# A scheduler's prices and positions chosen anew in a one-core attention and feed-forward kernel

## The chip, the cores and the metric

The kernel runs on one core of a Trainium2 chip. The core has a matrix engine (TensorE, PE in the profile), a vector engine (VectorE, DVE), a scalar engine (ScalarE, ACT), a general engine (GpSimd, POOL) and a sync engine (SyncE, SP) that here issues nearly all DMA transfers. Each engine works through its own queue of instructions in a fixed order, and semaphores tie the queues together. The metric is device time in microseconds (us) of one execution; the less the better.

## The reference

Linear attention with a norm is followed by a feed-forward layer with softplus:

```python
# q, k, v: (8, 8, 576, 64) float32: batch, heads, positions, head width
kv = np.einsum('bhsd,bhse->bhde', k, v)
out = np.einsum('bhsd,bhde->bhse', q, kv)
rms = np.sqrt(np.mean(out * out, axis=-1, keepdims=True) + 1e-06)
attn = out / rms * g_norm
x = attn.transpose(0, 2, 1, 3).reshape(4608, 512)
h = x @ w_in                                  # w_in: (512, 2048), float64
g = np.maximum(h, 0.0) + np.log1p(np.exp(-np.abs(h)))
return g @ w_out                              # w_out: (2048, 512), float64
```

## The kernel before

Tokens are cut into 36 tiles of 128. For each of the 8 batches `kv_of` loads K and V in pieces and multiplies them (line 691), and for each tile `rows` transposes q (line 771 on PE for the first two batches, line 746 on DVE for the others), multiplies it with kv (line 715), squares on ACT, sums on DVE (719), takes the root on POOL (722, 723) and scales on DVE (727). The result is transposed back on PE (733) for the first 12 tiles and on DVE for the others, and stored to DRAM.

Matrix products of the feed-forward layer keep float32 precision by splitting each operand into three pieces of a shorter format, so that a product is three passes. x is split by `split` (ACT line 635, DVE 638 and 641). Weights come as float64, 512 KB a piece; DVE and ACT turn them into float32 (lines 429 to 459) and split them (496 to 524, where lines 520 and 521 are on PE for the first four chunks). The 2048 hidden columns are 16 chunks of 128.

The feed-forward work has two forms. The narrow form (`step`) takes blocks of three tiles (384 tokens): 12 blocks, four chunks each for the first four blocks and six for the rest, 64 steps. A step is one first product (line 858, 12 matmuls), softplus and split on ACT and DVE (880, 882, 869, 873), and three second products (line 865, 3 matmuls each). The wide form (`wide_step`) does the remaining chunks over 512 tokens at a time in 48 steps, by a scheme that needs seven products where eight would be needed (line 1060, 6 matmuls each), with ACT copies and one DVE addition (line 1109) between them and eight second products (line 1130, 3 matmuls each). Its inputs are prepared by `units_of` (loads at line 989, kept at 970), its weights by `both`.

None of this is issued in program order. Every operation is first a task: `add` names its engine, a price in ns, the tasks that it waits for, buffers taken and given back, a transfer size for DMAs and a position. `Plan.order` plays the tasks through a simple model of the engines and the DMA queue. At each turn an engine looks at the tasks that could start within SOON of its first and takes the one with the lowest position; the resulting starts give the order in which all instructions are issued. The prices and positions therefore make no work, but set the order in every queue. What else the model has:

- HANDOVER: what passes between the end of a task on an engine and the start of one that waits for it; SWITCH: what PE pays extra from one kind of visit (rows, kv, all the rest) to another.
- `behind`: a gate. A load waits until the first product at or before that position has been done. A negative gate is none.
- `spare`: while the seventh first product has not started, PE's gaps of 400 ns or more are filled with matmuls that compute nothing (line 1224).
- P0 to P7: the positions. FETCH and CONVERT are the first eight weights' loads and conversions, P4 the tiles, P5 the batches' kv and q, P1 and P2 the later weights, P3 the offsets inside a wide step, P6 the unit loads.

Four load buffers of 256 KB hold K and V (ring e); one buffer each holds a raw piece of w_in and of w_out; two PSUM banks (ring h) hold the narrow first products.

## Time and profile before

| | |
|---|---|
| Median of 3 runs (lowest to highest) | 869.35 us (868.46 to 869.48) |
| The profiled execution | 869.26 us, span 867.5 us |
| Instructions | 17041 |
| DMA | 167.07 MB, mean 193 GB/s over the span |
| Granted TensorE clock, mean | 1.000 |

The span runs from the first instruction to the last. "Busy" is the time in which an engine executes at least one instruction; matmuls overlap, so the mean duration of one is longer than the pitch at which they start. PEld is the weight load of PE, which overlaps the matmuls. Line numbers are those of the kernel before. An "idle before" names what ended the wait.

### The profile page before, as it was taken

Reading aid. Unit: us, or ns where it says so; the run is one execution under the profiler, and the core shown is the slowest. Engines: PE = TensorE matmul, PEld = TensorE weight load, DVE = VectorE, ACT = ScalarE, POOL = GpSimd, SP = SyncE. Lnnn points to the kernel's source line nnn. Section 1 sums busy time; section 2 is a strip of 40 time slices with the busy share of each in tenths; the row PEclk is TensorE's granted clock in tenths of the full one; section 3 lists DMA queues with packets and bytes.
Section 4 is the critical chain, followed back from the end, with each engine's and each line's share of the span. In section 5 each row is a group of like instructions: output and inputs, shape, how many; then the busy total and the mean of one; then the engine's idle time right before and its main releaser. Section 6 shows DMA issues by size and latency. Waiting matters only on the chain.

```text
span 867.5 us, 17041 instructions
## 1 busy us (share of the span) xinstructions
PE 853.9 (98%) x6464; PEld 760.3 (88%) x6464; DVE 704.4 (81%) x995; ACT 521.3 (60%) x980; POOL 76.6 (9%) x79
## 2 busy tenths in 40 slices
PE   7899999999999999999999999999999999999998
PEld 5678888898888999989999999998999899999996
DVE  7888898888788879798887798878788666788873
ACT  6866664445444467766667655654868555566654
POOL 0342223111113200000000000000000000000000
PEclk9999999999999999999999999999999999999999
DMA  9998998779773655436645546545364752777764
GB/s 278 285 242 230 244 262 255 172 224 234 211 188 114 180 175 166 145 108 209 210 156 164 168 151 205 188 144 170 122 201 140 230 165 91 241 236 241 242 190 126
DMA packets 239778, 167.07 MB, mean 193 GB/s; under 512 B 106320, under 2 KB 198736, under 8 KB 239696
## 3 DMA queue, kind: packets, MB, share of 16 engines
q1 hardware_dynamic: 239392, 165.86, 64.5%
q8 instruction: 50, 0.82, 0.4%
q14 instruction: 32, 0.26, 0.1%
q10 hardware_dynamic: 304, 0.13, 0.1%
HBM read 112.98 MB, written 52.95 MB: 191 GB/s over the span
## 4 chain that ended last, share of the span: by engine, by line
PE 94%; DVE 1%; ACT 1%; POOL 0%; issue 0%; ACTq 0%; DVEq 0%
PE banks L1130 31%; PE banks L1060 28%; PE banks L865 16%; PE banks L858 15%; PE banks L715 2%; PE banks L691 2%; PE banks L733 0%; DVE units L638 0%; DVE half L727 0%; PE banks L1224 0%; POOL roots L723 0%; DVE units L641 0%; DVE roots L719 0%; DVE m L459 0%; ACT units L635 0%
## 5 line engine op out<-in xcount | busy, mean ns | idle before, releaser
L1130 PE MATMUL banks<-pieces,gv 128*128 128x512 f32 x768 | 239.9, 394 | 0.0
L1130 PEld LDWEIGHTS banks<-pieces,gv 128*128 128x128 f32 x768 | 133.5, 189 | 18.4
L1130 PE MATMUL banks<-pieces,g_False 128*128 128x512 f32 x384 | 149.4, 389 | 0.0
L858 PE MATMUL banks<-units,pieces 128*128 128x384 f32 x768 | 145.4, 337 | 0.0
L865 PE MATMUL banks<-pieces,gv 128*128 128x512 f32 x576 | 144.9, 396 | 0.0
L858 PEld LDWEIGHTS banks<-units,pieces 128*128 128x128 f32 x768 | 135.5, 188 | 4.8
L865 PEld LDWEIGHTS banks<-pieces,gv 128*128 128x128 f32 x576 | 106.1, 188 | 20.3
L1060 PEld LDWEIGHTS banks<-units,pieces 128*128 128x128 f32 x840 | 112.8, 190 | 6.8 <-ACT banks L1105 0.4
L1060 PE MATMUL banks<-units,pieces 128*128 128x256 f32 x840 | 117.1, 282 | 0.0
L880 ACT ACTIVATE half<-banks 128x384 f32<-128x384 f32 x64 | 31.4, 491 | 98.2 <-PE banks L858 98.0
L1120 DVE TENSOR_TENSOR gv<-g_True,gv 128x1024 fp32r<-128x1024 f32 x47 | 57.5, 1223 | 37.8 <-ACT gv L1117 37.8
L1130 PEld LDWEIGHTS banks<-pieces,g_False 128*128 128x128 f32 x384 | 72.2, 188 | 15.9
L1060 PEld LDWEIGHTS banks<-units,w 128*128 128x128 f32 x504 | 67.8, 190 | 3.9 <-ACT banks L1105 0.2
L1060 PE MATMUL banks<-units,w 128*128 128x256 f32 x504 | 70.7, 282 | 0.0
L723 POOL TENSOR_TENSOR roots<-roots,half 128x8 f32<-128x8 f32 x36 | 62.3, 1731 | 3.0
L1123 DVE SCALAR_TENSOR_TENSOR g_False<-gv 128x1024 fp32r<-128x1024 f32 x47 | 57.6, 1225 | 1.5
L1109 DVE TENSOR_TENSOR g_True<-banks,g_True 128x512 f32<-128x512 f32 x48 | 33.1, 690 | 30.5 <-PE banks L1060 24.5
L1087 ACT ACTIVATE g_True<-banks 128x256 f32<-128x256 f32 x96 | 36.6, 382 | 32.8 <-PE banks L1060 32.2
L1023 DVE TENSOR_TENSOR units<-loads,units 128x1024 fp32r<-128x1024 f32 x42 | 51.2, 1219 | 6.3 <-ACT units L1020 6.3
L925 ACT ACTIVATE m<-banks 128x512 f32<-128x512 f32 x72 | 42.1, 595 | 19.8 <-PE banks L1130 13.8
L1026 DVE SCALAR_TENSOR_TENSOR units<-units 128x1024 fp32r<-128x1024 f32 x42 | 51.4, 1224 | 1.8
L869 DVE TENSOR_TENSOR gv<-half,gv 128x384 fp32r<-128x384 f32 x64 | 35.4, 553 | 20.6 <-ACT gv L882 19.9
(115 smaller groups left out, 1260.5 us busy)
## 6 DMA issues: line engine op xcount, KB each, us to landing
loads<-x SPq DMA_DIRECT2D x180, 128.0 KB, 2.6
part<-m SPq DMA_DIRECT2D x72, 256.0 KB, 2.9
m<-part SPq DMA_DIRECT2D x72, 256.0 KB, 3.2
loads<-form SPq DMA_DIRECT2D x45, 256.0 KB, 3.2
form<-loads SPq DMA_DIRECT2D x36, 256.0 KB, 3.0
raw<-in_moe_w_in_dram SPq DMA_DIRECT2D x16, 512.0 KB, 4.5
loads<-in_k_dram SPq DMA_DIRECT2D x32, 256.0 KB, 4.1
loads<-in_v_dram SPq DMA_DIRECT2D x32, 256.0 KB, 4.4
```

The costliest lines, as they stand in the source:

```text
L723: nc.gpsimd.tensor_tensor(out=r.tile, in0=r.tile, in1=half, op=ALU.pow)
L858: nc.tensor.matmul(hp, lhsT=w_in.tile[:, i, kd * P:(kd + 1) * P], rhs=xv.tile[:, i, kd], start=(m == 0), stop=(m == 3 * KD - 1))
L865: nc.tensor.matmul(mine[i].tile, lhsT=gv.tile[:, m, i * P:(i + 1) * P], rhs=w_out.tile[:, m], start=(c == cs[0] and m == 0), stop=(c == cs ...
L869: nc.vector.tensor_tensor(out=gv.tile[:, 1], in0=g.tile, in1=gv.tile.bitcast(F32)[:, 0], op=ALU.subtract)
L925: a = add("ACT", 690 if ph == LAST else 600, lambda: nc.scalar.activation(new(ot, [P, d_model]), bank.tile, func=AF.Copy, scale=scale if p ...
L1023: nc.vector.tensor_tensor(out=part_of(1, F32R), in0=xl.tile if m > 1 else xl.tile[:, 0], in1=part_of(0), op=ALU.subtract)
L1026: nc.vector.scalar_tensor_tensor(out=part_of(2, F32R), in0=part_of(1), scalar=-RADIX, in1=part_of(0), op0=ALU.mult, op1=ALU.add)
L1060: nc.tensor.matmul(place(q), lhsT=w[:, m, at:at + P], rhs=dst.tile[:, m, v, kd] if u < 6 else dst.tile[:, m, kd], start=(u == 0 and not m ...
L1087: nc.scalar.activation(dst, src, func=AF.Softplus, scale=1.0 + E)
L1120: nc.vector.tensor_tensor(out=gvt(1, F32R), in0=gt(), in1=gvt(0), op=ALU.subtract)
L1123: nc.vector.scalar_tensor_tensor(out=gt(F32R), in0=gvt(1), scalar=-RADIX, in1=gvt(0), op0=ALU.mult, op1=ALU.add)
L1130: nc.tensor.matmul(mine[i].tile, lhsT=(gvt(m, F32R) if m < 2 else gt(F32R))[:, c, i * P:(i + 1) * P], rhs=outs[c].tile[:, m], start=fresh ...
```

## The change

The planner's model of prices changes, and the positions are replaced. No task is added or taken away, apart from the number of fill matmuls that the planner chooses.

- HANDOVER gives way to two figures: a task occupies its engine for `busy`, which on ACT and DVE is less than its price, and is seen by others after `lag`; REACH is added on the side of the waiting engine.
- SWITCH knows four forms of dense visit (mm1, mm2, prod, all) and prices each change between them and rows or kv. PE prefers to stay in a form by 0.5 of a position.
- Prices of PE tasks, SP issues (460 ns for most) and transfer sizes are new, and SOON is 60 instead of 150, the fill 260 instead of 400.
- A new list P8 gives positions of their own to the split and the overflow sum of the first eight weights, the stores of the first 12 tiles and the second products of the first 16 narrow steps.

The diff, cut to its core (price changes of the same kind are left out; of the lists only P0, P3, P4, P5 and P6 are shown; P1, P2 and P7 are replaced in the same manner, and P8 has 44 entries):

```diff
-    HANDOVER = {"PE": 250, "ACT": 120, "DVE": 120, "POOL": 150, "SP": 0}
+    OVERLAP = {"ACT": (250, 60, 105), "DVE": (200, 40, 90)}
+    SEEN = {"PE": 0, "ACT": 33, "DVE": 33, "POOL": 34, "SP": 0}
+    REACH = {"PE": 190, "ACT": 0, "DVE": 0, "POOL": 55, "SP": 0}
     READY = {"PE": 2500, "ACT": 2500, "DVE": 4000, "POOL": 2500, "SP": 700}
-    SWITCH = {("all", "rows"): 90, ("all", "kv"): 90, ("rows", "all"): 250, ("kv", "all"): 250, ("rows", "kv"): 140, ("kv", "rows"): 140}
+    SWITCH = {("prod", "mm2"): 17, ("mm1", "mm2"): 30, ("mm2", "mm1"): 30, ("rows", "kv"): 60, ("kv", "rows"): 100}
+    for form in ("mm1", "mm2", "prod", "all"):
+        SWITCH.update({("rows", form): 260, ("kv", form): 290, (form, "rows"): 10, (form, "kv"): 10})
+    STAY = 0.5
-    LANDING, FILLED = 3500, 60000
+    LANDED, LANDING, FILLED = 1300, 3500, 60000
+    QUEUED = 3000
-    SOON = 150
+    SOON = 60
...
+        limit, short, long = self.OVERLAP.get(engine, (0, 0, 0))
+        t.busy = ns - (long if ns > limit else short)
+        t.lag = ns - t.busy + lag + self.SEEN[engine]
...
-                        at = max(at, dma_free - 2500)
+                        at = max(at, dma_free - self.QUEUED)
...
-                at, t = min(options, key=lambda o: (o[1].pos, o[0]))
+                at, t = min(options, key=lambda o: (o[1].pos - (self.STAY if engine == "PE" and o[1].kind == "all" and o[1].form == form else 0), o[0]))
...
-            engine_free[t.engine] = at + t.ns
-            t.end = at + t.ns + self.HANDOVER[t.engine]
+            engine_free[t.engine] = at + busy
+            t.end = at + busy + t.lag
...
-                t.end = dma_free + (self.LANDING if dma_free > self.FILLED else 2000)
+                t.end = dma_free + (self.LANDING if dma_free > self.FILLED else self.LANDED)
...
-                    u.ready = max([a.end for a in u.after] + ([u.follows.start] if u.follows else []), default=0)
+                    u.ready = max([a.end + self.REACH[u.engine] for a in u.after] + ([u.follows.start] if u.follows else []), default=0)
...
-    P0 = [-45.94, -26.77, -11.8, 0.28, -29.91, -5.64, -2.86, 3.84, -103.4, -98.98, -69.3, -76.66, -68.5, -24.67, -23.22, -34.97, 8.15, -43.02, 7.47, 9.69, 7.18, 18.16, -12.1, 4.75, 1.0, 106.19, 31.3, 6.28, 7.19, 5.22]
-    P4 = [-30.17, -6.08, 16.93, -33.9, -22.35, -28.91, -17.33, -7.12, -18.68, -2.69, 0.62, 2.73, -7.38, -1.86, 1.1, 1.72, 5.22, -13.65, 3.22, 0.88, 43.88, 43.95, -0.17, -0.32, 44.8, 40.82, -20.17, -6.56, 6.41, 10.03, -10.73, 0.23, 2.8, 0.42, -9.48, -5.03]
-    P5 = [1.24, -5.69, -2.28, -3.57, 1.72, 0.53, 6.68, -5.83, 3.01, -2.95, 3.35, 1.4, -6.96, 0.27, -5.34, -2.29]
+    P0 = [-68.7, -102.34, -44.82, -198.78, -249.41, -62.35, -115.05, 6.21, -525.68, -256.69, -299.97, -218.24, -570.6, -112.98, -68.54, -94.85, -20.21, -104.06, 52.6, 12.02, 30.74, 101.38, -89.91, 0.87, 2.46, 290.7, 63.96, 11.88, 7.87, 7.29]
+    P4 = [-106.62, -49.32, -12.94, -239.17, -63.65, -156.56, -38.04, -130.43, -253.55, -40.59, 8.15, -36.8, 140.03, -108.31, -11.51, 403.76, 8.82, -40.31, 56.72, -0.01, 294.4, 87.55, 118.45, -23.98, 191.1, 161.79, 101.83, -115.05, 18.29, -158.32, -176.64, 0.8, -4.24, -184.6, -64.73, 82.92]
+    P5 = [-65.91, -22.31, -22.19, 41.72, -93.2, -155.53, 98.26, 0.78, 50.55, -63.11, -38.66, 4.6, -5.42, 20.99, -30.64, -2.0]
-    P6 = [1.05, 6.24, 4.29, 4.08, -1.52, -2.85, 1.21, -0.34, 3.11, 3.1, -1.07, -0.73, -0.88, 9.99, 5.7, 5.69, 0.13, 0.46]
+    P6 = [18.97, 22.66, -6.96, -0.88, -33.45, -44.23, -110.04, 16.54, 29.17, -20.75, 14.92, -72.25, -181.54, 3.37, -1.25, -197.59, -239.43, -207.09]
...
-    P3 = [2.14, 2.48, 6.41, -16.53, 0.86, 2.79, 4.01, -16.44, 3.79, 3.96, 2.19, 1.79, 0.72, 1.35, 1.55, -1.03]
+    P3 = [7.03, 2.4, 10.2, -70.67, 2.74, -26.0, 4.18, -42.87, -107.53, 2.93, -129.46, 1.88, -15.26, -256.2, 14.29, 9.63]
...
-        f = add("SP", 450, fetch, (), fetch_pos, [raw], size=1800, behind=behind)
+        f = add("SP", 460, fetch, (), fetch_pos, [raw], size=2250 if of_out else 1750, behind=behind)
...
-            divide(j, w, ready, pos, c < 4)
+            divide(j, w, ready, pos + (P8[j] if c < 4 else 0), c < 4)
...
-            b2 = add("PE", 500, less_by_pe, [e], pos, [bank])
+            b2 = add("PE", 334, less_by_pe, [e], pos, [bank], lag=92)
...
-            lds = [add("SP", 500, lambda src=src, s=s, load=load: load(src, s), (), pos - EARLY[6] + 0.5 * p + (P7[2 * (5 * b + p) + of_v] if b < 2 else 0), [s], [],
-                       650 if tail else 850, behind=pos - 5.5) for of_v, (src, s) in enumerate(((k, ks), (v, vs)))]
+            lds = [add("SP", 460, lambda src=src, s=s, load=load: load(src, s), (), pos - EARLY[6] + 0.5 * p + (P7[2 * (5 * b + p) + of_v] if b < 2 else 0), [s], [],
+                       640 if tail else 930, behind=pos - 5.5) for of_v, (src, s) in enumerate(((k, ks), (v, vs)))]
...
-            last = add("PE", 470, run, lds + ([last] if b < 2 else []), pos + 0.5 * p, [bank] if p == 0 else [], [ks, vs], kind="kv",
+            last = add("PE", 467, run, lds + ([last] if b < 2 else []), pos + 0.5 * p, [bank] if p == 0 else [], [ks, vs], kind="kv", lag=209,
...
-        a = o_task = add("PE", 484, out_rows, turned + need, x_pos(t - second), [o], [qT], kind="rows", follows=rows_done.get(t - 1))
+        a = o_task = add("PE", 515, out_rows, turned + need, x_pos(t - second), [o], [qT], kind="rows", follows=rows_done.get(t - 1), lag=240)
...
-        a = add("PE", 2100, mm1, x_split[n] + factors_done[0, c] + [m for _, m in mm1s[-1:]] +
+        a = add("PE", 2092, mm1, x_split[n] + factors_done[0, c] + [m for _, m in mm1s[-1:]] +
                 (factors_done[1, ORDER[s - 2][1]] if s > 1 else []), s, [h],
-                ([xv] if c == cs[-1] else []) + ([w_in] if s == last_step[c] and c != 4 else []))
+                ([xv] if c == cs[-1] else []) + ([w_in] if s == last_step[c] and c != 4 else []), lag=41, form="mm1")
...
-            a2 = add("PE", 700, lambda i=i: mm2(i), [a] + factors_done[1, c] + [mm2s.get(i)], s + 1.5,
+            a2 = add("PE", 684, lambda i=i: mm2(i), [a] + factors_done[1, c] + [mm2s.get(i)], s + 1.5 + (P8[28 + s] if s < 16 else 0),
                      [mine[i]] if c == cs[0] else [],
-                     [gv] + ([w_out] if s == last_step[c] and not kept else []))
+                     [gv] + ([w_out] if s == last_step[c] and not kept else []), form="mm2")
...
-            return add("PE", 710, lambda: product(u, q), unit_done[ph, n, u] + forms_done[p][f] + list(after), pos, take, give,
-                       follows=follows)
+            return add("PE", 716, lambda: product(u, q), unit_done[ph, n, u] + forms_done[p][f] + list(after), pos, take, give,
+                       follows=follows, lag=83, form="prod")
...
-    plan.spare = ("h", warm, 400, mm1s[6][1])
+    plan.spare = ("h", warm, 260, mm1s[6][1])
```

## The prediction

> **What bounds the kernel now.** I read the page first: the engines' busy shares and the shares of the chain that ended last.
>
> ```profile
> span 867.5 us, 17041 instructions
> ...
> PE 853.9 (98%) x6464; PEld 760.3 (88%) x6464; DVE 704.4 (81%) x995; ACT 521.3 (60%) x980; POOL 76.6 (9%) x79
> ...
> PE 94%; DVE 1%; ACT 1%; POOL 0%; issue 0%; ACTq 0%; DVEq 0%
> ```
>
> TensorE (PE) is busy 98% of the span and is 94% of the chain. But busy says nothing of useful: next the busy times by stage (columns: window, length, PE, PEld, DVE, ACT, POOL busy with counts, granted clock, DMA share, GB/s), and behind them the first row again for line 1224 alone, the fill matmuls, which compute nothing.
>
> ```profile
> 0.00:80.00 80.00, 70.17 (x904) 54.20 (x905) 67.93 (x119) 54.51 (x106) 24.15 (x29) 1.00 0.96 256
> 80.00:300.00 220.00, 220.00 (x2104) 196.76 (x2103) 188.32 (x323) 111.99 (x223) 52.46 (x50) 1.00 0.78 212
> 300.00:850.00 550.00, 550.00 (x3390) 497.90 (x3389) 443.53 (x547) 348.91 (x643) 0.00 (x0) 1.00 0.56 178
> 850.00:867.50 17.50, 13.71 (x72) 11.41 (x70) 4.60 (x8) 5.92 (x11) 0.00 (x0) 1.00 0.40 124
> ```
> ```profile
> 0.00:80.00 80.00, 18.86 (x52) 10.77 (x52) 1.00 0.96 256
> ```
>
> From 80 to 850 us PE has no idle at all. In the first 80 us it is idle 80 - 70.17 = 9.8 us and fills for 18.86: 28.7 us without use. The last 3.8 us are the last copy and store.
>
> Is the packed part at its least? The chain gives the pitch of each kind of visit (start, us, what):
>
> ```profile
> 192.74 2.10 PE banks L858 x12
> 194.84 2.08 PE banks L865 x9
> ...
> 442.42 2.87 PE banks L1060 x24
> 445.30 2.75 PE banks L1130 x12
> ```
>
> So the narrow first product (768 matmuls) takes 64 x 2.10 = 134.4 us, the narrow second one (576) 64 x 2.08 = 133.1, the wide first one (2016) 84 x 2.87 = 241.1, the wide second one (1152) 96 x 2.75 = 264.0. PE's timeline gives the small visits, and what changing costs:
>
> ```profile
> 108.38 2.27 PE L858 MATMUL banks<-units,pieces 128*128 128x384 f32 x12
> 110.58 1.16 PE L715 MATMUL banks<-early,w 64*64 64x64 f32 x64
> 111.67 4.42 PE L865 MATMUL banks<-pieces,gv 128*128 128x512 f32 x18
> 115.93 2.27 PE L858 MATMUL banks<-units,pieces 128*128 128x384 f32 x12
> 118.13 1.15 PE L691 MATMUL banks<-loads 128*64 128x64 f32 x32
> 119.21 0.69 PE L715 MATMUL banks<-early,w 64*64 64x64 f32 x32
> 119.83 2.35 PE L858 MATMUL banks<-units,pieces 128*128 128x384 f32 x12
> ```
>
> Start to start, two tiles of rows (x64) take 1.09, two kv visits (x32) 1.08: 36 rows make 19.6, 40 kv visits 21.6; 22 transposes at some 0.38 and 8 pairs of lines 520 and 521 at some 0.55 (the same timeline, before 80 us) 12.8. The sum is 826.6. With 1.6 us before the first matmul and 3.8 behind the last it is 832.0 of 867.5. Of the 35.5 left, 27.1 are the start's (28.7 less that 1.6). The other 8.4 are changes of visit: the dense visits beside a small one take 0.10 too much on either side (108.38 to 110.58 is 2.20, not 2.10; 111.67 to 115.93 is 4.26, not 4.16), so 0.2 for each of some 43 stays of small work, 18 of them after 80 us.
>
> What holds the start? DVE works 67.93 of the first 80 us, and its own timeline shows it packed:
>
> ```profile
> 35.44 0.68 DVE L719 TENSOR_REDUCE roots<-half 128x8 f32<-128x512 f32 x1
> 36.03 0.68 DVE L442 SCALAR_TENSOR_TENSOR m<-sq,m 128x512 f32<-128x512 bf16 x1
> 36.63 0.68 DVE L727 TENSOR_TENSOR half<-banks,roots 128x512 f32<-128x512 f32 x1
> ```
>
> These start every 0.60, while the planner before charged 690 and a handover of 120. DVE's least before the last second product of the first block: 8 weights x (0.43+0.69+0.69+0.43+0.69+0.69+0.72) = 34.7, 3 tiles x 4 x 0.69 = 8.3, 4 steps x 1.1 = 4.4, after the first landing at 4.36: 51.8 us. That product ended near 79; the rest of DVE's time went to later tiles. Of its 12.1 us idle, 2.6 lie before that landing, 9.5 behind it, in pieces of 0.1 to 1.3 waiting for ACT, PE and POOL. The first dense visit shows how a fixed order loses time: its tile was split by 40.7, but PE takes two small visits and six fills, 42.96 to 44.44, first.
>
> **The change part by part.** No instruction is added or removed but fills; what changes is the order in each queue, computed from new prices and positions. Which order comes out can't be read from the diff, so each part is bounded.
>
> Prices of DVE and ACT: they are now occupied 40 to 105 ns less than an operation lasts. That is what the rows above show (0.60 for 0.68). Over the 119 DVE operations of the first 80 us the old plan charged some 0.09 too much each, 10.7 us, and so gave DVE's queue and PE's fills an order for a slower start. What a truer order can win by packing alone is DVE's 9.5 us of idle time; what it can lose is one weight's way, 5.8 us from issue to landing. I take a gain of 4.5, half of the idle time: no row says how many pieces had other ready work.
>
> Fills: 260 instead of 400 ns, so shorter gaps are filled and there will be more than 52 of them. A fill at pitch 0.23 delays what is ready behind it. Between the six before the first dense visit gone (-1.5) and a dozen more that come late (+2.8) I take 0; the cover is that DVE, not PE, is late there.
>
> Changes: to rows and back is charged 270 instead of 340, to kv and back 300. Four stays merged or split at 0.2 give -0.8 to +0.8; I take 0, since the price hardly moves.
>
> Gates and transfers: worked from the new positions, K/V loads of batches 4, 5 and 6 lose their gates (behind narrow steps 10, 13, 23 before, now none), and so do q of batch 3 and many loads of units. They can come into the start, past the weights on SP. Only four load buffers of 256 KB exist: 1.05 MB, 4.1 us at the 256 GB/s above, is the most. I take 0, as their positions (39, 46, 76) stand behind every weight fetch of the start (-68 at the latest); ends 0 and +4.1. SP issues as many DMAs as before, at some 0.46 each; the larger transfer prices move no data.
>
> Packed part, 80 to 850: 0. A gain is excluded beyond the changes; a loss is the second rival. Tail: 0.
>
> Sum: -4.5 against the profiled execution's 869.26 (span 867.5 and 1.8 around it; 0.09 below the median) gives 864.8, against the median 864.9. I say **865**, and 0.2% (1.7 us) is what a measurement can tell from no change.
>
> **The rivals.**
>
> *A load held on SP in the start (slower, chance 0.17).* SP issues in order. A load placed early whose buffer comes free late holds the weights and K/V behind it, then DVE, then PE. For it: the open gates, a landing now priced 1300 instead of 2000 before 60 us, the start's DMA share of 0.96. Against: SP's longest wait in the first 80 us is 2.9 us, and PE waits for K/V only 0.2 to 1.7 at a time. It decides once a weight is later than DVE's idle pieces hide, about 1 us. Price: a landing of 4.1 to 5.8 us less that, some 4: 873. [...]
>
> *The wide steps lose their cover (slower, 0.11).* Positions of the second products and of the product after DVE's addition move by up to 250 steps. That addition (0.69 us at line 1109, and ACT's copies at some 0.37) stands between two products, and second products of the step before hide it. If they are used up too soon, PE waits some 0.2 us in each of 48 steps: 9.6 us, 879. For it: 550 us rest on this order. Against: in each 10.5 us step 5.5 us of second products cover some 1.5 us. It decides below two of them between the last two products.
>
> *No change (0.10).* The start is held by transfers, at 0.96 of the DMA engines; another order moves the same bytes: 869. Against: DVE waits for a landing 1.8 us in all. [...]
>
> *More than packing (faster, 0.16).* DVE's work for later tiles is put off, toward its 51.8 us: as the start then gives up to twice the 4.5, some 859.
>
> **How the numbers follow.** My forecast has 0.46, with its own range 861 to 867.5. Faster: 0.46 + 0.16 = 0.62; same 0.10; slower 0.17 + 0.11 = 0.28. The range runs from 858, which leaves out half the bigger gains (0.08), to 876, which leaves out the wide-step case (0.11).
>
> **What would show it.** Right: the first dense visit before 44.4 us; fills and idle together under 25 us in the first 80; DVE over 70 us busy there; no idle PE from 80 to 850; some 18 stays after 80. Wrong: PE idle at K/V or weights in the start, or gaps at lines 1060 and 1130 in the wide steps.

## The result and the profile after

The changed kernel is slower: 875.35 us median of 6 runs (875.15 to 875.73) against 869.41 us for the kernel before (6 runs beside it, 868.46 to 870.48). The ratio is 1.0068, 95% interval 1.0055 to 1.0081. The forecast was 865.0, range 858 to 876: the time fell inside the range, but on the other side of no change.

Line numbers of the changed kernel are those of the kernel before plus 12 wherever this text needs them: 691 is 703 (kv), 715 is 727 (rows), 733 is 745 (turn of x), 858 is 870 (narrow first product), 1224 is 1236 (fill). The profiled execution took 875.72 us. From the page of the changed kernel, the span, the busy shares and the chain:

```profile
span 873.9 us, 17082 instructions
PE 861.9 (99%) x6501; PEld 764.2 (87%) x6501; DVE 688.8 (79%) x995; ACT 515.5 (59%) x980; POOL 80.8 (9%) x79
PE 92%; DVE 2%; ACT 2%; DMA 1%; POOL 1%; SPq 1%; issue 1%; DVEq 0%; ACTq 0%
```

PE is busy for 8.0 us more, DVE for 15.6 us less. There are 37 fills more (89 for 52), each a matmul and a weight load, and 33 semaphore instructions less, which makes the 41 instructions more. Busy times by stage (window, length, then PE, PEld, DVE, ACT, POOL busy with counts, granted clock, DMA share, GB/s), and the first window again for the fills alone (line 1236):

```profile
0.00:80.00 80.00, 73.92 (x809) 58.48 (x810) 62.83 (x114) 50.65 (x100) 20.78 (x25) 1.00 0.94 242
80.00:300.00 220.00, 217.94 (x2207) 193.93 (x2207) 180.21 (x316) 111.79 (x221) 60.00 (x54) 1.00 0.78 213
300.00:850.00 550.00, 550.00 (x3380) 494.89 (x3379) 437.02 (x555) 342.90 (x642) 0.00 (x0) 1.00 0.56 178
```
```profile
0.00:80.00 80.00, 27.14 (x89) 17.34 (x89) 1.00 0.94 242
```

In the first 80 us PE is idle for 6.08 us and fills for 27.14: 33.2 us without use, where it was 28.7. From 80 to 300 us another 2.06 us are idle, where there were none. Together that is 6.6 us, and the last product ends 6.4 us later than before (870.09 against 863.71). So nearly the whole loss is in the start and just behind it; the wide steps, from 300 to 850 us, have no idle time, as before.

What the start hangs on shows in PE's timeline (start, busy, line, operation, idle time before and its releaser): K/V visits of batch 0, the first rows, one K/V visit of batch 1, the first dense visit.

```profile
14.82 0.69 PE L703 MATMUL banks<-loads 128*64 128x64 f32 x16
20.03 0.69 PE L703 MATMUL banks<-loads 128*64 128x64 f32 x16
24.68 0.69 PE L703 MATMUL banks<-loads 128*64 128x64 f32 x16
28.01 1.16 PE L727 MATMUL banks<-early,w 64*64 64x64 f32 x64
45.45 0.69 PE L703 MATMUL banks<-loads 128*64 128x64 f32 x16 [0.66 <-DMA loads<-in_v_dram]
50.29 2.03 PE L870 MATMUL banks<-units,pieces 128*128 128x384 f32 x10
```

The first three lines are the second to fourth K/V visits of batch 0. The same visits, the first rows and the first dense visit in the kernel before:

```profile
9.57 0.69 PE L691 MATMUL banks<-loads 128*64 128x64 f32 x16
...
15.32 0.69 PE L691 MATMUL banks<-loads 128*64 128x64 f32 x16
...
19.30 0.69 PE L691 MATMUL banks<-loads 128*64 128x64 f32 x16 [1.69 <-DMA loads<-in_k_dram]
...
21.44 1.16 PE L715 MATMUL banks<-early,w 64*64 64x64 f32 x64
...
44.44 2.28 PE L858 MATMUL banks<-units,pieces 128*128 128x384 f32 x12
```

The K/V visits are 4.7 to 5.4 us later, the first rows 6.57, the first dense visit 5.85. The queue of SP shows the reasons (start, time the issues took, line, tile, count):

```profile
10.53 2.59 SPq L773 DMA_DIRECT2D w<-in_q_dram  x4
13.16 2.25 SPq L773 DMA_DIRECT2D early<-in_q_dram  x4
15.54 0.43 SPq L692 DMA_DIRECT2D loads<-in_k_dram  x1
...
17.72 0.50 SPq L692 DMA_DIRECT2D loads<-in_v_dram  x1
...
31.52 3.99 SPq L625 DMA_DIRECT2D early<-in_q_dram  x2
35.57 5.39 SPq L773 DMA_DIRECT2D w<-in_q_dram  x2
41.05 0.45 SPq L810 DMA_DIRECT2D x<-w  x1
41.62 0.99 SPq L692 DMA_DIRECT2D loads<-in_v_dram  x2
```

Four q loads (eight DMAs, for two half tiles and two whole ones) go ahead of the last K piece (15.54) and V piece (17.72) of batch 0. In the kernel before, all K/V pieces of that batch are issued by 12.21 us:

```profile
10.14 0.45 SPq L680 DMA_DIRECT2D loads<-in_k_dram  x1
10.65 0.98 SPq L680 DMA_DIRECT2D loads<-in_v_dram  x2
11.82 0.34 SPq L418 DMA_DIRECT2D g<-in_moe_w_out_dram  x1
12.21 0.42 SPq L680 DMA_DIRECT2D loads<-in_k_dram  x1
```

The eight issues take 4.84 us of SP's time. The K piece behind them then lands 3.23 us after its own issue, while the one issued at 12.21 in the kernel before took 6.96; so its place behind these issues made it late more than a full queue of transfers did. The second K/V visit is late for a reason of its own: its V piece is issued at 8.79 us (before at 4.30), behind two weight pieces (5.93 and 7.71). The V piece at 17.72, too, stands behind two of them (16.08 and 17.30).

Later, from 32 to 41 us, three issues take 3.45, 3.53 and 1.81 us; the median of the 810 issues on SP in this trace is 0.43. The V piece behind them is issued at 41.62 and lands at 45.41, where PE has been waiting for it.

Behind 80 us there is one new gap of more than 0.3 us: the turn of x at 89.55.

```profile
89.55 0.63 PE L745 MATMUL banks<-ident_r,half 128*128 128x128 f32 x4 [1.45 <-DVE half L739]
```

Two sums of the planner belong to this picture; they are plans, not measurements. The changed kernel's planner, with its new prices, ends the last product of its own order at 866.2 us. Given the order of the kernel before, the same prices end it at 871.7. So by its own prices the change gains 5.5 us. On the chip the old order ended at 863.7, 8.0 ahead of that plan, and the new one at 870.1, 3.9 behind it.

### The profile page after: what moved, and what is told of

It reads as the page before. It is cut to its first block, busy times and chain, and to the rows that moved or that the text cites. A ratio compares the mean times of both kernels' runs of the same rounds, so it can differ in the third digit from the quotient of the medians.

```text
span 873.9 us, 17082 instructions
## 1 busy us (share of the span) xinstructions
PE 861.9 (99%) x6501; PEld 764.2 (87%) x6501; DVE 688.8 (79%) x995; ACT 515.5 (59%) x980; POOL 80.8 (9%) x79
## 4 chain that ended last, share of the span: by engine, by line
PE 92%; DVE 2%; ACT 2%; DMA 1%; POOL 1%; SPq 1%; issue 1%; DVEq 0%; ACTq 0%
PE banks L1142 30%; PE banks L1072 28%; PE banks L877 14%; PE banks L870 14%; PE banks L703 2%; PE banks L727 2%; PE banks L1236 1%; POOL roots L735 1%; SPq L773 1%; PE banks L745 0%; DMA loads<-in_v_dram 0%; DMA raw<-in_moe_w_in_dram 0%; PE banks L783 0%; DVE units L650 0%; DVE half L739 0%
## 5 line engine op out<-in xcount | busy, mean ns | idle before, releaser
L870 PEld LDWEIGHTS banks<-units,pieces 128*128 128x128 f32 x768 | 134.9, 188 | 5.3 <-ACT half L892 0.6
L1072 PE MATMUL banks<-units,pieces 128*128 128x256 f32 x960 | 134.5, 283 | 0.0
L1072 PEld LDWEIGHTS banks<-units,pieces 128*128 128x128 f32 x960 | 126.6, 191 | 8.8 <-ACT banks L1117 3.6
L735 POOL TENSOR_TENSOR roots<-roots,half 128x8 f32<-128x8 f32 x36 | 64.2, 1782 | 3.0
L1032 ACT ACTIVATE units<-loads 128x1024 fp32r<-128x1024 f32 x42 | 44.4, 1057 | 19.8 <-PE banks L1072 18.2
L1072 PE MATMUL banks<-units,w 128*128 128x256 f32 x384 | 54.6, 283 | 0.0
L1072 PEld LDWEIGHTS banks<-units,w 128*128 128x128 f32 x384 | 50.8, 191 | 2.9 <-ACT banks L1117 1.5
```

What stands on the lines that cost most here:

```text
L735: nc.gpsimd.tensor_tensor(out=r.tile, in0=r.tile, in1=half, op=ALU.pow)
L870: nc.tensor.matmul(hp, lhsT=w_in.tile[:, i, kd * P:(kd + 1) * P], rhs=xv.tile[:, i, kd], start=(m == 0), stop=(m == 3 * KD - 1))
L1032: nc.scalar.activation(part_of(0, F32R), xl.tile if m > 1 else xl.tile[:, 0], func=AF.Copy, scale=DOWN)
L1072: nc.tensor.matmul(place(q), lhsT=w[:, m, at:at + P], rhs=dst.tile[:, m, v, kd] if u < 6 else dst.tile[:, m, kd], start=(u == 0 and not m ...
```

## The experiments

All runs keep the kernel's tasks and prescribe their order as a list of task numbers, -1 for a fill, so that one place can be changed while every other queue stays as it was. The list is read in the planner:

```diff
-            best = None
-            for engine, tasks in ready.items():
+            best, fixed = None, []
+            if self.listed:
+                n = self.listed.pop(0)
...
+                    t = self.tasks[n]
...
+                best = (at, t)
+            for engine, tasks in ready.items() if best is None else ():
```

With it line numbers grow by 32 over the kernel that the list is put into. Below only the edit of the list is shown. Each run stands beside runs of the kernel before on the same chip, with a median of 869.15 to 869.94 us, and its ratio is to those.

### Where the time is lost: the start of one order, the rest of the other

```diff
-LISTED = old[all]
+LISTED = old[start < 90 us] + new[the rest]
```

> Every queue begins with the order of the kernel before (its plan up to 90 us, that is the first 86 us on the chip) and goes on in the order of the changed kernel. If the loss sits in the start, as the two traces place it (excess over the least pitch from 0 to 100 us: 32.5 before, 38.1 after; from 100 us on 10.1 and 11.0), this takes about 870.3. If the rest carries it, it stays at 875.

```diff
-LISTED = new[all]
+LISTED = new[start < 90 us] + old[the rest]
```

> The reverse: every queue begins with the order of the changed kernel (its plan up to 90 us, 93 us on the chip) and goes on in the order of the kernel before. Loss in the start: about 874.5, with the rest 0.9 better than in the changed kernel. Loss in the rest: 869.

Measured: old_start 880.61 us, ratio 1.0124 (1.0103 to 1.0145); new_start 887.80, ratio 1.0211 (1.0193 to 1.0229). The totals decide nothing, since the seam costs more than the question. PE's waits from 80 to 125 us, old_start first, then new_start (line waited at, releaser, us in total, times, longest):

```profile
PE banks L909 <- ACT gv L926: 6.3, 1, 6.3
```
```profile
PE banks L777 <- DVE half L771: 13.6, 2, 12.1
```

The first dense visit, which comes long before the seam, goes with the order of the start: 46.07 us in old_start, 49.91 in new_start. Joining halves of two plans tells little: each half counts on what the other does.

### Do the 37 fills more cost the time?

```diff
-LISTED = new[all]
+LISTED = new[all, without the fills behind the 20th]
```

> The changed kernel with its order, but only its first 20 fill matmuls (to 9.7 us); the other 69 are left out. Theory 'fills': planned at 260 ns they fill the planned gaps exactly, PE is never idle from 9 to 35 us and cannot run ahead of the plan when data come early, as it did before; without them the first rows (28.0 us) start 2 to 3 us earlier and the time falls to 872 to 873. Theory 'load order': rows wait for K and V, which are issued late, and the fills only pass the time: 875, with PE idle in their place. A third possibility: PE's clock falls without fills, and the time rises by 1 to 4.

Measured: 878.22 us, ratio 1.0101 (1.0083 to 1.0118), 2.9 us slower than the changed kernel, as the third possibility had it. The first 80 us in its profile:

```profile
0.00:80.00 80.00, 62.56 (x730) 50.25 (x731) 60.65 (x110) 48.67 (x96) 19.62 (x25) 0.83 0.91 235
```

The granted clock is 0.83 there, where the changed kernel has 1.00, and the visits in the slow stretches take longer (a K/V visit 1.12 us instead of 0.69). So the fills are worth having as a whole, and that they are the whole loss falls. Whether they hold PE up at full clock, this run can't tell, because the clock fell with them. The changed kernel's own trace says that in places they do. The V piece issued at 17.72 us landed at 22.29, but its visit starts at 24.68, since ten fills stand ahead of it:

```profile
21.89 2.86 PE L1236 MATMUL banks<-ident_r 128*128 128x512 f32 x10
```

The second to fourth K/V visits start 1.6, 1.3 and 2.4 us after their last piece has landed; in the kernel before it is 0.13 us at most. From 18 to 52 us the fills are 21% of the chain that ended last. No run took such fills away at full clock, so what they cost is open.

### The two reasons on SP, and the gap at 89.55

```diff
-... 538 539 489 399 449 452 ...
+... 489 399 449 452 538 539 ...
```

(538 and 539 are q of batch 2, 449 and 452 the V pieces.)

> The changed kernel with the first two q loads of batch 2 (32 partitions, pieces of 128 bytes; issued at 31.5 and 32.1) moved behind the V loads that the first block's PE order waits for. Theory 'held SP': SP's issues from 32 to 41 us, which took 3.5, 3.5 and 1.8 instead of 0.5, fall back to 0.5 to 1, the K/V visit at 45.4 and the first dense visit at 50.3 come 1.3 to 2 us earlier, and the time is 873 to 874. Rival: the hold has another cause (the queue is full of the other loads) and the time stays at 875.

Measured: 875.84 us (874.91 to 876.77), ratio 1.0072 (1.0053 to 1.0090). SP's long issues in front of the V pieces are gone, and the first dense visit comes 1.13 us earlier:

```profile
37.56 0.90 SPq L724 DMA_DIRECT2D loads<-in_v_dram  x2
```
```profile
49.16 2.38 PE L902 MATMUL banks<-units,pieces 128*128 128x384 f32 x12
```

The last product ends 0.82 us earlier in the profiled execution (869.27), but the median does not move. The held queue is worth about 1 us of the first dense visit, and in the time nothing is seen of it.

```diff
-... 552 1086 ...
+... 1086 552 ...
```

> The changed kernel, its order kept as a list, with one move on TensorE: the turn of x at 89.55 us (line 745), for which TensorE stood idle for 1.45 us, goes behind the dense first product that follows it. The whole computation is there. Theory 'the idle time is a loss': the idle time goes and nothing takes its place, so the time falls by 1.0 to 1.5 us, to 873.9 to 874.4. Rival 'the turn feeds what comes next': the tile is turned 2.3 us later, the visits that need it wait, and the time is the same within 0.5 us or up to 1.8 us longer (877.2), the last being what the planner's own sum says of this order.

Measured: 876.14 us, ratio 1.0080 (1.0063 to 1.0097). The gap at the turn is gone, but the rows behind it now wait:

```profile
89.33 0.60 PE L777 MATMUL banks<-ident_r,half 128*128 128x128 f32 x4
90.61 0.69 PE L759 MATMUL banks<-early,w 64*64 64x64 f32 x32 [0.68 <-ACT w L841]
```

By the pitches of the forecast, this order loses 3.1 us from 80 to 100 us, the changed kernel 2.7. The turn feeds what comes next; moved, its idle time only changes place.

### The order of the loads alone, in the kernel before

```diff
 28(weight)
+400 458 461
 376(K) 377(V) 380(V) 42(weight) 379(K)
-400 458 442 461
+442
```

> The kernel before, its order kept as a list, with one move: three loads of q tiles (the three that it issues after 13 us) go ahead of the last three K/V loads of batch 0. Nothing else changes, and the whole computation is there. In the changed kernel the same loads stand in that order: the K/V visits of batch 0 there end with starts at 20.03, 24.68 and 25.73 us, where they start at 15.32, 19.30 and 19.79 before. Theory 'order of the loads': the late K/V pieces are a main part of the longer start. Then the first rows visit (21.44 before) and the first dense first product (44.44) come 2 to 4 us later, and the time rises by 2 to 4 us, to 871.5 to 873.5. Rival 'cover': the rows visits have time to spare before the dense work starts, so the first dense visit stays within 0.7 us of 44.44 and the time within 1 us of 869.4. Second rival: the q tiles, loaded earlier, free the queue later on and the start gets shorter by about 1 us.

Measured: 872.09 us (871.13 to 873.65), ratio 1.0037 (1.0024 to 1.0050), 2.9 us slower. The third K/V visit waits, the first rows come at 25.44 (before 21.44), the first dense visit at 48.32 (before 44.44), the last product at 867.54 (before 863.71):

```profile
18.31 1.12 PE L723 MATMUL banks<-loads 128*64 128x64 f32 x16 [2.43 <-DMA loads<-in_v_dram]
```

Three q loads (one whole tile, two half ones) ahead of the last four K/V pieces push the start by 3.9 us, and all of it arrives at the end. Their six issues take 3.7 us of SP's queue (10.78 to 14.46), and the K piece behind them is issued at 14.56 (10.14 before). But this visit takes 1.12 us instead of 0.69, and the windows show why (18 to 24 us, columns as above):

```profile
18.00:24.00 6.00, 5.62 (x52) 4.44 (x54) 2.81 (x5) 1.87 (x3) 0.00 (x0) 0.50 0.96 318
```

The clock was granted at 0.50. So the loss could be the clock's. Nine fills in front of that visit tell:

```diff
 ...
+-1 -1 -1 -1 -1 -1 -1 -1 -1
 378(kv)
```

> The order of kv_behind (three q tile loads ahead of the last three K/V loads of batch 0) with nine fills more, ahead of the K/V visit at 18.31 us for which TensorE stood idle for 2.43 us. The whole computation is there. In kv_behind the granted clock was 0.50 from 18 to 24 us and 0.86 to 26. Theory 'the loads': the K piece for the next visit landed at 22.31 us there and the visit started at 22.36, so the slow clock lay beside a wait; at full clock the first dense visit comes 0.4 to 0.8 us earlier than 48.32, and the time is 2 to 3 us above that of the kernel before, 871.3 to 872.5. Rival 'the clock': with the clock at 1.00 the first dense visit comes back to 44.4 to 45.5 and the time to within 1 us of 869.4.

Measured: 873.09 us (871.56 to 874.30), ratio 1.0036 (1.0023 to 1.0048). Two windows of its profile and the next K/V visit:

```profile
18.00:22.00 4.00, 2.24 (x22) 1.57 (x22) 0.55 (x2) 1.00 (x2) 0.00 (x0) 1.00 1.01 338
22.00:26.00 4.00, 3.90 (x51) 3.18 (x54) 3.64 (x6) 1.86 (x5) 0.00 (x0) 0.57 1.03 292
```
```profile
22.10 1.04 PE L723 MATMUL banks<-loads 128*64 128x64 f32 x16 [1.86 <-DMA loads<-in_k_dram]
```

The clock is at 1.00 until 22 us, and PE now stands idle for the K piece (1.86 us) instead of running slowly up to it; the fall, to 0.57 from 22 to 26 us, comes one visit later. The first dense visit (48.12) and the time stay. Nor did the one execution of kv_behind with a mean clock of 1.000 come back; it took 871.13 us. The loads are the cause, the clock is beside it.

### What else is as tight: a weight later, a K piece sooner, fills gone

```diff
-42(weight) 379(K) 400 458
+379(K) 400 458 42(weight)
```

> The order before, as a list, with one move: the fourth weight load (512 KB, 11.82 us on SP) goes behind the K piece and the two q tile loads that follow it. The whole computation is there. The old prices plan 2.5 us for it, the new ones 0.1. Theory 'the start is tight': 2 to 4 us slower, 871.5 to 873.5, the first dense visit later by as much. Rival 'only the K/V pieces decide': the K piece comes earlier, the weight's lateness is hidden, and the time is within 1 us of 869.3 or below it.

Measured: 871.66 us (10 runs, 870.96 to 873.49), ratio 1.0023 (1.0011 to 1.0035), 2.0 us slower. K/V come earlier (17.78), but PE then waits for the parts of the late weight, and the first dense visit is 1.74 us later (46.18):

```profile
22.17 0.67 PE L553 MATMUL banks<-pieces,gv 128*128 128x512 f32 x1 [2.42 <-ACT pieces L541]
```

```diff
-42(weight) 379(K)
+379(K) 42(weight)
```

> The order before, as a list, with one move: the last K piece of batch 0 (issued at 12.21 us, landed at 19.17, and waited for by TensorE for 1.69 us) goes one place ahead, before the weight load issued at 11.82. The whole computation is there. The old prices plan 0.6 us more for it, the new ones no difference. Theory 'the start is tight': the weight that is now later takes back what the K piece wins: first dense visit 0 to 1 us later, time 869 to 870.5. Rival 'only the K/V pieces decide': the visit of K/V at 19.30 comes 1 to 1.7 us earlier, the first dense visit too, and the time is 867.6 to 868.3.

Measured: 869.68 us (10 runs, 868.46 to 871.50), ratio 0.9995 (0.9984 to 1.0007). The K/V visit comes 1.31 us earlier, and a weight's second line waits in its place; the first dense visit stands at 44.44 as before:

```profile
17.99 0.69 PE L723 MATMUL banks<-loads 128*64 128x64 f32 x16
...
21.29 0.49 PE L553 MATMUL banks<-pieces,gv 128*128 128x512 f32 x1 [0.64 <-ACT pieces L541]
```

So in the start before, K/V pieces and weights are balanced: each of the two made later costs 2 to 3 us, and the K piece made sooner gains nothing. Whether the q tiles are as tight was not tried.

```diff
 478(rows)
--1 -1 -1 -1 -1 -1
 1024(first dense visit)
```

> The order before, as a list, without the six fills ahead of the first dense visit (42.96 to 44.44 us). The whole computation is there. The prediction took it that these six hold the visit back: then it comes 1.0 to 1.5 us earlier and the time falls by as much, to about 868. Rival, by the tile's second split, which ends at 45.0 us: the visit starts earlier but waits inside for that split, so that what follows it starts within 0.3 us of before, and the time is the same within 0.5 us.

Measured: 868.98 us (10 runs, 867.94 to 870.59), ratio 0.9986 (0.9976 to 0.9996). The visit starts earlier, stops inside for the split of tile 2, and the next turn of x comes at 45.29 (before 46.56):

```profile
41.88 1.68 PE L890 MATMUL banks<-units,pieces 128*128 128x384 f32 x8
43.99 0.97 PE L890 MATMUL banks<-units,pieces 128*128 128x384 f32 x4 [0.43 <-DVE units L673]
```

Of those 1.27 us, 1.06 were there already at the fourth K/V visit (18.24 for 19.30 us), ahead of the edit, because its K piece landed earlier in this execution. That leaves 0.2 for the fills themselves, by this one execution. This is the only order with an interval below 1; the 0.7 us are less than the 0.2% that counts here.

### Is it the prices? Six orders searched under them

The next six take an order's first 100 us and move single tasks about at random, keeping a move where the planner's sum of the whole order gets smaller. They differ in the start and in the prices that judge: old order and new prices (search_old, search_old_b), new order and new prices (search_new), old order and old prices (old_prices, old_prices_b), old order and the mean of both (both_prices).

```diff
-LISTED = old[all]
+LISTED = searched[start < 100 us] + old[the rest]
```

> The order before, kept as a list, whose first 100 us are rearranged by a search: tasks are moved one at a time, and a move is kept where the changed kernel's new prices (not the old ones) make the planned end earlier; 34 TensorE tasks and 51 loads change places, with 54 fills instead of 52. The whole computation is there. By the new prices the last product of the order before ends at 871.7 us, of this one at 869.6, of the changed kernel at 866.2, and the first dense visit is planned 2.4 us earlier than in the order before (45.6 instead of 48.0). Theory 'the prices are true enough, the order before only needs a better start': the time falls by about 2 us, to 867.3. Rival 'the plan's last microseconds are not real': a plan tuned to these prices has no slack left on the chip, so that the gain is lost or turns round, as in the changed kernel: 869 to 873.

> The same search from the same order with other random moves: the same planned end (869.6), the first dense visit planned at 45.8 us, 34 TensorE tasks and 52 loads moved. The whole computation is there. Theory 'prices true enough': as the other one, 867.3, and within 0.5 us of it. Rival 'the last microseconds are not real': 869 to 873, and since the two differ in what they leave without slack, they lie more than 0.5 us apart.

> The changed kernel's order, kept as a list, its first 100 us rearranged by the same search under the same new prices: planned end 864.3 instead of 866.2, first dense visit planned at 46.2 instead of 48.9 us, 52 fills instead of 89, 34 TensorE tasks and 56 loads moved. The whole computation is there. Theory 'prices true enough': 1.9 us less than the changed kernel, 873.4, and with the chip's lag of 4 us behind the plan unchanged the order before stays the better one. Rival 'the last microseconds are not real': the lag behind the plan grows by as much as the plan wins, 875 to 878. A third: the changed kernel lost its time by the late loads of its start alone, and a first dense visit 2.7 us earlier gives 872.5 or less.

> The order before, its first 100 us rearranged by the same kind of search as the three searches under the new prices (one task at a time, the same reach), but judged by the old prices: the planned last product comes 0.6 us earlier under the old prices (875.9 to 875.2) and 1.1 us earlier under the new ones (871.7 to 870.6). 33 TensorE tasks and 51 loads change places, as many as in those searches; 53 fills. The whole computation is there. Theory 'slack': the old prices charge every operation of DVE and ACT about 0.1 us too much and a landing 0.7 us more than the new ones do, and so an order that is good under them keeps room for what the chip adds; the rearranged order loses nothing: 868 to 870. Rival 'any rearranging costs': what made those three searches 6.8, 9.9 and 16.1 us slower than the kernel before was that so many tasks were moved away from a tuned order; then 874 to 880 here.

> The same search under the old prices with other random moves: 0.6 us earlier under the old prices, 0.5 us later under the new ones (872.2); 35 TensorE tasks and 49 loads moved, 52 fills. The whole computation is there. Theory 'slack': 868 to 870. Rival 'any rearranging costs': 874 to 880. Third, 'the new prices rank the orders': this one is 1.6 us slower than the other search under the old prices.

> The same search with the mean of the planned ends under the old and the new prices as its judge: 0.6 us earlier under the old ones, 2.1 us earlier under the new ones (869.6, the same as the two searches from the order before reached under the new prices alone); 26 TensorE tasks and 52 loads moved, 52 fills. The whole computation is there. Theory 'slack': since the old prices hold it back, it keeps what the other two lost, and is 0.6 to 2.1 us faster than the kernel before: 867.3 to 868.8. Rival 'any rearranging costs': 874 to 880. Third, 'the new prices are wrong on this start whatever else is asked for': as the searches under the new prices, 876 or more.

All six came out slower than the kernel before. The three searches under the new prices fell outside every range that I had given for them, and both_prices between its three. Planned and measured end of the last product (us in the profiled execution), with the time:

| order | planned, old prices | planned, new prices | end on the chip | median | ratio (interval) |
|---|---|---|---|---|---|
| before | 875.9 | 871.7 | 863.7 | 869.41 | 1 |
| changed kernel | 940.6 | 866.2 | 870.1 | 875.35 | 1.0068 (1.0055 to 1.0081) |
| kv_behind | 878.1 | 871.9 | 867.5 | 872.09 | 1.0037 (1.0024 to 1.0050) |
| w_later | 878.3 | 871.8 | 865.4 | 871.66 | 1.0023 (1.0011 to 1.0035) |
| search_old | 884.1 | 869.6 | 876.1 | 879.40 | 1.0116 (1.0094 to 1.0138) |
| search_old_b | 880.5 | 869.6 | 870.8 | 876.23 | 1.0074 (1.0058 to 1.0091) |
| search_new | 929.6 | 864.3 | 876.9 | 885.60 | 1.0181 (1.0156 to 1.0206) |
| old_prices | 875.2 | 870.6 | 870.3 | 877.60 | 1.0100 (1.0074 to 1.0125) |
| old_prices_b | 875.2 | 872.2 | 873.4 | 877.44 | 1.0096 (1.0079 to 1.0113) |
| both_prices | 875.2 | 869.6 | 866.9 | 872.48 | 1.0041 (1.0026 to 1.0056) |

"Prices true enough" falls at once: search_new, the best plan of all, is the slowest here. The new prices plan 0.2 us for kv_behind and 0.1 for w_later, which cost 2.9 and 2.0. My theory of slack falls too: the two orders searched under the old, more generous prices lost 8.3 to 8.5 us, within what its rival had foretold, and they lie 0.2 us apart where the new prices said 1.6. Since the old prices lose as much, the six do not show that the new ones are worse; that any wide rearranging of this start costs, whatever judges it, fits them as well. What stands is simpler. On the chip these orders end between 8.0 us ahead of the new plan and 12.6 behind it, while the new plans themselves differ by 8; the old prices put the changed kernel's order at 940.6, 70 us too high. So a planned gain of 0.6 to 5.5 us lies inside the plan's error. Two waits that search_new meets: a load on SP, issued at 80.50 us, has waited 5.6 us for a K/V buffer, and a rows visit at 67.51 waits 2.9 for its tile (SP's waits, then PE's timeline):

```profile
SPq L724 <- PE banks L735: 5.8, 2, 5.6
```
```profile
67.51 0.69 PE L759 MATMUL banks<-early,w 64*64 64x64 f32 x32 [2.86 <-DVE half L771]
```

In their profiled executions all six have windows of 2 us with a granted clock of 0.50 to 0.56 in the first 80 us, which no plan knows. They do not explain the loss: two executions of search_old with a mean clock of 1.000 took 877.91 and 878.17 us. both_fed puts 29 fills into the idle pieces of both_prices:

```diff
 ...
+-1 (x15)
 372(kv)
 ...
```

> The order of both_prices with 29 fills more, placed ahead of the five visits before which TensorE had stood idle for 0.60 to 3.63 us in its first 45 us. The whole computation is there. In both_prices the granted clock was 0.50 to 0.75 from 8 to 16 us and 0.50 to 0.66 from 28 to 32 us, together 5.1 us of full speed lost. Theory 'the clock ate what the plan won': at full clock the visits behind these idle pieces take their normal time, and the time falls by 1 to 3 us from 872.5, to 869.5 to 871.5, or to 867 to 868 if the planned gain of 0.6 to 2.1 us comes out at last. Rival 'the clock fell where TensorE was waiting anyway': the time stays within 0.7 us of 872.5.

Measured: 875.55 us (873.22 to 876.90), ratio 1.0058 (1.0039 to 1.0076), not faster than both_prices but 3.1 us slower, which neither forecast had. The two executions with a mean clock of 1.000 took 873.22 (the profiled one) and 873.25, the four others, at 0.998, 875.41 to 876.90; why is open. From 8 to 16 us, both_prices and then both_fed:

```profile
8.00:16.00 8.00, 6.53 (x46) 5.18 (x47) 6.98 (x13) 4.15 (x8) 0.00 (x0) 0.57 1.09 338
```
```profile
8.00:16.00 8.00, 8.00 (x62) 5.94 (x60) 7.43 (x14) 4.60 (x10) 0.00 (x0) 1.00 1.07 306
```

The clock is back at 1.00 and nothing is won, even in this execution: in this stretch it had fallen where PE was waiting anyway.

## Why the prediction was wrong

*What bounds the kernel.* Right: the start decides. Nearly the whole difference lies in the fills and idle time of the first 90 us.

*Start order, -4.5: the step that failed.* I took half of DVE's 9.5 us of idle time as the gain of a truer order, on the ground that truer prices make a better order. DVE's work in the first 80 us fell to 62.83 us instead of rising over 70, and the first dense visit came 5.85 us later. That this is near the other end that I had given, a weight's way of 5.8, is chance: what came late were K/V pieces, by their places in SP's queue and, in part, by fills ahead of their visits. The missing thought was that the order before might stand better on the chip than the new prices say. It did, by 8.0 us, and the new prices, asked about both orders, put them 5.5 us apart in the wrong direction.

*Gates and transfers, 0.* I looked at the batches whose gates open and at the weights, and found them far behind. What moved was inside batch 0: four q loads ahead of its last K/V pieces, and weights ahead of two V pieces. Such a swap with three q loads costs 2.9 to 3.4 us in the kernel before, 3.9 at the first dense visit. That it is the greater part of the 5.9 in the changed kernel is argued from the same late visits, not shown: there the second visit is late by the weights, fills hold three visits back, and the places depend on each other.

*Fills, 0: not shown.* 37 more, 8.3 us more of them, and PE's idle time 3.7 us less. Fifteen of them took 3.80 us (11.02 to 14.82), some 0.25 each; priced at 260 ns instead of 400 they fill a planned gap nearly to its end, and PE can't start early when data land ahead of the plan. At three K/V visits that came to 1.3 to 2.4 us, and I had put it at 0 because DVE was late. Against that, 69 of them taken away cost 2.9 us more, at a granted clock of 0.83 in the first 80 us; what they add up to stays open. My -1.5 for the six before the first dense visit rested on a misread row: the split that ended at 40.7 belongs to tile 3. Tile 2 is split from 42.91 to 45.0, and without the six fills the visit stops inside; in that profile they are worth 0.2.

*Changes of visit, 0.* 20 stays of small work after 80 us for 17, and 0.9 us more over the least pitch from 100 us on (11.0 for 10.1): at the edge of its bounds. *Packed part and tail, 0:* right; no idle time from 300 to 850, 3.8 us behind the last product. The 2.06 us between 80 and 300 us I had at 0; the greater part is the gap at 89.55.

*The rivals.* The nearest was "a load held on SP in the start", 873 with a chance of 0.17. Loads are late there, and in the kernel before a weight or K/V pieces made later cost 2 to 3 us, near its price of 4. But its mechanism, a buffer that comes free late, is a small part: in the first 30 us the longest wait on SP that the profile shows is 1.7 us, and the pieces are late by the order of issue. (For the first of the long issues at 32 us the profile names the turn of x on PE, 3.1 us, which does not read that buffer.) "The wide steps lose their cover" is out. "No change", by transfers, is out too, but the mean of 256 GB/s over 80 us hid that the rate changes from one stretch to the next. The kernel before from 14 to 18 us, while the K piece takes 6.96 us to land, and the changed kernel from 14 to 22:

```profile
14.00:18.00 4.00, 3.10 (x25) 1.89 (x24) 3.40 (x6) 2.74 (x6) 0.00 (x0) 1.00 1.03 343
```
```profile
14.00:18.00 4.00, 4.00 (x32) 2.61 (x31) 3.96 (x8) 2.50 (x6) 0.00 (x0) 1.00 1.02 236
18.00:22.00 4.00, 4.00 (x37) 3.28 (x37) 2.22 (x4) 3.48 (x7) 0.00 (x0) 1.00 1.01 340
```

When that piece is issued, the five loads ahead of it, 1.8 MB, have not landed; at 343 GB/s they take up to 5.3 us, an estimate from these two figures. At 236 GB/s the changed kernel's K piece, issued at 15.54, landed after 3.23 us, so the order of issue held it. Over the first 50 us the changed kernel moves less: 242 GB/s against 273. The changed kernel moved 374 GB/s from 10 to 12 us, so 343 is no ceiling here. "More than packing" is out.

*The range* held the time by luck: its upper end, 876, stood between the prices of two rivals, 873 and 879, and neither of their mechanisms explains the time.

## What to carry to other kernels

A planner's prices can be revised after the trace and still choose a worse order: put the old order through the new prices first, and if the chip beats that plan by more than the planned gain, the gain is inside the model's error. In a start that waits for loads, read the queue of loads piece by piece, with the time that the issues take, and the GB/s in windows of a few microseconds, not over the stage; one piece made sooner can gain nothing while the others stay. Compare landing and use of each piece: work that only fills time can stand between them. Change such an order one place at a time, and measure each.

## What the runs showed of the hardware

In windows of 2 us over the first 130 us, the granted clock was 1.00 throughout in the profiled executions of the kernel before, six_gone, k_sooner, the changed kernel, q_later, turn_later and both_fed. In the others it was lower for stretches, down to 0.50. The full-speed time lost there, worked out from these windows (the length of each times what its clock lacks of 1.00), is 1.7 us (w_later, kv_fed), 3.4 (kv_behind, search_old_b, old_prices), 5.1 (search_old, search_new, both_prices), 6.8 (old_prices_b, new_start), 8.5 (old_start) and 13.7 (few_fills). Taken as 0.50 throughout, single stretches come to some 3.4 us (w_later, between 22 and 26 us), 6.8 (kv_behind, 16 and 26), 10.2 (few_fills, 12 and 24), 13.6 (new_start, 100 and 116) and 17.1 (few_fills, 32 and 52).

Four of these stretches stand beside a wait of PE. In few_fills PE is idle for 3.24 us ahead of the visit at 14.61, and the clock is 0.80 from 12 to 14 us and 0.50 from 14 to 22. In kv_behind it is idle for 2.43 us ahead of the visit at 18.31, with 0.93 from 16 to 18 and 0.50 from 18 to 24. In w_later it is idle for 2.42 us ahead of the line at 22.17, with 1.00 until 22 and 0.58 from 22 to 24. In kv_fed it is idle for 1.86 us ahead of the visit at 22.10, with 1.00 until 22 and 0.57 from 22 to 26. Behind the 1.69 us of idle time ahead of 19.30 in the kernel before, the clock stayed at 1.00. What decides between these cases, no run here shows.

An issue on SP's queue, 0.43 us in the median of the changed kernel, took 3.45 and 3.53 us at 32 and 36 us, with the transfers at 206 GB/s between 30 and 50 us. In q_later the four issues behind the V pieces, the two moved q loads first, took 4.96 us together (38.51 to 43.47). What holds the queue there was not found.
